# Splitting attention operands earlier and weights later in a float32 attention + MoE kernel

## The chip, the cores and the metric

The kernel runs on one core of a Trainium2 chip. The metric is the device time of one execution in microseconds (us); the kernel before takes 1088.51 us (median of 3 runs, 1087.3 to 1088.69).

## The reference, cut to what matters

Eight batches of eight heads attend over 32 global and 512 local positions with head dimension 64. The global queries see every position; a local query sees the 32 global positions and a band of 32 positions on either side. The result, 4352 rows of 512, goes through a two-layer network with a sigmoid gate. Everything is float32, and the weights come in as 64-bit floats.

```
s_g = scale * matmul(q_g, k_all.T);  out_g = matmul(softmax(s_g), v_all)
s_ll = where(abs(i - j) <= 32, scale * matmul(q_l, k_l.T), -1e9)
a_l = softmax(concat([scale * matmul(q_l, k_g.T), s_ll]))
x = concat([out_g, matmul(a_l, v_all)])        # (8*544, 512)
h = x @ w_in                                   # w_in: 512 x 2048
out = (h * (1 / (1 + exp(-h)))) @ w_out        # w_out: 2048 x 512
```

## The kernel before, in words

**Two kinds of product.** TensorE can multiply float32 operands as they are ("whole"), which the hardware does as two instructions for one matmul, or it can multiply rounded operands (type `F32R`). For the second kind each operand is split into a rounded high part and the rest, and a product is the sum of three: high by high, high by low, low by high. A whole operand is ready when it has been loaded. A split one first needs a cast on ScalarE (ACT) and a subtraction on VectorE (DVE) or GpSimd (POOL).

**Attention.** There are 128 local steps, numbered k: one step is a pair of heads for 128 queries of one batch, four steps make one tile of 128 rows. Each step loads q and k (`st_load`, L285) and v (`st_vload`, L293), splits them (`st_split`, L301; `st_vsplit`, L316), forms scores and softmax (`st_scores`, L327), transposes the probabilities (`st_turn`) and multiplies by v (`st_out`, L404). Steps with k below `KF` (24) are whole: `st_split` and `st_vsplit` return at once, the scores are one matmul for each head, and the probabilities are transposed where they stand. From `KF` on the scores are three products (for k below `ND` = 28), the probabilities are first moved by a DMA within SBUF into the tile `rr` (L365), of which there is one, and are then transposed; the transposed ones are split into `pt_hi` (ACT, L389) and `pt_lo` (DVE, L390), with the columns of the global queries added on POOL (L400, L401), and the product with v has six matmuls for a head where the whole form has two (each two-part). For k below 28 the subtractions for k (`klo`, L310) and v (`vlo`, L323) are on POOL. The global queries have steps of their own (`g_load`, `g_scores`, `g_soft`, `g_turn`), whole for the first two batches.

**The two-layer network.** The rows go through in 12 blocks of 2 or 3 tiles (`SIZES`). A block has 16 slices f of the hidden dimension: `first_layer(n, f)` forms h for 128 hidden units, ACT and DVE apply the gate, and one slice later `second_layer(n, f)` adds into the output. Block 0 is whole, with float32 weights `w_32`; the blocks from 1 on use the split weights `w_hi` and `w_lo`. A half slice of weights comes in by `load_weights` (L164): a DMA of 64-bit words into one of eight buffers `raw_w` (L171), a conversion on ACT (L179), and two integer operations on DVE (L181, L182). `split_weights(f)` (L185) makes the high part with two casts on ACT (L192) and the low part with two subtractions on POOL (L193); the tile of `w_lo[f]` takes the place of `w_32[f - 1]`, so the subtraction waits until block 0 is done with that.

**What sets the order.** The order of TensorE (PE) is written out: the planner gives each part of a step a due time, and `fill` hands out the parts that are due between the matmuls of the slices, so that attention for the next block runs inside the current one. Before block 0 the program issues the scores of steps 0 to 9, the transposes of steps 0 to 8 and the outputs of steps 0 to 7; block 0 then holds the outputs of steps 8 to 19, block 1 goes on with step 20. The other engines and the DMA queue of SP are ordered by the scheduler of the language, which takes the program order as priority and a simulated time for readiness, so an instruction can be placed well ahead of where the program has it. Each engine then works its list strictly in order.

**Places of the change.** `KF` (L41), `FIRSTW` (L46: the step from which, up to step 7, one `load_weights` is put at each step; what is still missing is loaded from slice 0 on, `LOOK` = 5 slices ahead), the call of `split_weights(f)` at the end of `second_layer` in block 0 (L592), and the main loop (L606).

Of the kernel before, what the change touches and what calls it, by code (L numbers as in the profile page):

```python
# [28 lines left out]
NCC, NF = DM // P, DFF // P  # L29
# [8 lines left out]
SIZES = (2, 3, 3, 3, 3, 3, 3, 3, 3, 3, 3, 2)  # L38
BUFS = dict(qk=2, raw=2, p=2, vraw=2, rr=1)
ND = 28  # L40
KF = 24  # L41
GF = 2
KP = 12
SCRATCH = 8
LOOK = 5
FIRSTW, PACE, WAT = 2, 1.0, -1.5  # L46

DUE = dict(load=-1.2, split=-0.5, vload=-0.6, vsplit=0.95, turn=1.6, out=2.2)
LAG = 2.25
# [9 lines left out]
def attention_moe_kernel(ctx: ExitStack, tc: tile.TileContext, qk0_in, qk_in, v_in, gqk, wts, out):  # L59
# [48 lines left out]
    def scratch(i, dtype, name):  # L108
        assert i not in taken
        return const.tile([P, 2 * DM], dtype, tag=f"wh{i}", name=name)  # L110


    probs = [const.tile([P, 2, 2 * P], F32, name=f"probs{i}") for i in range(BUFS["p"])]
    more = [scratch(SCRATCH - 1 - i, F32, f"probs{i}_") for i in range(2)]
    probs += [more[i // 2][:, DM * (i % 2) : DM * (i % 2 + 1)].rearrange("p (u j) -> p u j", u=2) for i in range(3)]
# [28 lines left out]
    def raw_tile(name, whole=False):  # L144
        some = SCRATCH - 4 not in taken
        i = next(homes) % (4 if some else 2) if whole else 0
        if i > 1:
            return scratch(SCRATCH - 1 - i, F32, name)
        if i:
            return work.tile([P, QW + KW], F32, tag="qk", bufs=BUFS["qk"], name=name)  # L150
        return raws.tile([P, QW + KW], F32, tag="raw", name=name)
# [10 lines left out]
    w_32, w_hi, w_lo, w_next = [], [], [], [0, 0]  # L162

    def load_weights():  # L164
# [4 lines left out]
        w = w_32[f][:, c0 : c0 + DM]  # L169
        raw = scratch(SCRATCH + (2 * f + c0 // DM) % (NF - SCRATCH), I32, f"raw_w{f}_{c0}")  # L170
        load = nc.sync.dma_start(out=raw, in_=wts[f, :, c0 : c0 + DM].bitcast(I32))  # L171
        if 2 * f + c0 // DM < NF - SCRATCH:
            tc.keep_in_program_order(load)
# [11 lines left out]
    def split_weights(f):  # L185
        taken.add(f)
        w_hi.append(const.tile([P, 2 * DM], F32R, tag=f"wh{f}", name=f"w_hi{f}"))
        w_lo.append(const.tile([P, 2 * DM], F32R, tag=f"ws{f}", name=f"w_lo{f}"))
        for c0 in range(0, 2 * DM, DM):
            sl = slice(c0, c0 + DM)  # L190
            hi, lo, w = w_hi[f][:, sl], w_lo[f][:, sl], w_32[f][:, sl]
            nc.scalar.copy(out=hi, in_=w)  # L192
            nc.gpsimd.tensor_tensor(out=lo, in0=w, in1=hi.bitcast(F32), op=ALU.subtract)  # L193
# [91 lines left out]
    def st_load(k, b, c, pr):  # L285
        raw = raw_tile(f"raw{k}", k < KF)
        if k < ND:
            nc.sync.dma_start(out=raw[:, : QW + W], in_=qk0_in[k])
        else:
            nc.sync.dma_start(out=raw, in_=qk_in[k - ND])  # L290
        tiles["raw", k] = raw

    def st_vload(k, b, c, pr):  # L293
        if k < KF and k % 2:
            vraw = two.tile([P, 2, 2, D], F32, tag="vhi" if k % 4 == 1 else "vlo", name=f"vraw{k}")
        else:
            vraw = raws.tile([P, 2, 2, D], F32, tag="vraw", bufs=BUFS["vraw"], name=f"vraw{k}")
        nc.sync.dma_start(out=vraw.rearrange("p a u d -> p (a u d)"), in_=v_in[b, c, pr])
        tiles["vraw", k] = vraw

    def st_split(k, b, c, pr):  # L301
        if k < KF:
            return
        raw = tiles.pop(("raw", k))
        qk, klo = qk_tiles(k)
        tiles["qk", k] = qk, klo
        if k < ND:
            n = QW + W
            nc.scalar.copy(out=qk[:, :n], in_=raw[:, :n])
            (nc.gpsimd if k < ND else nc.vector).tensor_tensor(out=klo[:, :n], in0=raw[:, :n], in1=qk[:, :n].bitcast(F32), op=ALU.subtract)  # L310
            return
        nc.scalar.copy(out=qk, in_=raw)  # L312
        (nc.gpsimd if k < ND else nc.vector).tensor_tensor(out=klo[:, :KW], in0=raw[:, QW:], in1=qk[:, QW:].bitcast(F32), op=ALU.subtract)
        nc.vector.tensor_tensor(out=qk[D:, :QW], in0=raw[D:, :QW], in1=qk[D:, :QW].bitcast(F32), op=ALU.subtract)

    def st_vsplit(k, b, c, pr):  # L316
        if k < KF:
            return
        vraw = tiles.pop(("vraw", k))
        vhi = two.tile([P, 2, 2, D], F32R, tag="vhi", name=f"vhi{k}")  # L320
        vlo = two.tile([P, 2, 2, D], F32R, tag="vlo", name=f"vlo{k}")
        nc.scalar.copy(out=vhi, in_=vraw)
        (nc.gpsimd if k < ND else nc.vector).tensor_tensor(  # L323
            out=vlo, in0=vraw, in1=vhi.bitcast(F32), op=ALU.subtract)
        tiles["v", k] = vhi, vlo

    def st_scores(k, b, c, pr):  # L327
        if k < KF:
            raw = tiles.pop(("raw", k))
# [3 lines left out]
        for u in range(2):  # L333
            o = s[:, u * W : (u + 1) * W]
            qs = slice(u * P, (u + 1) * P)
            if k < KF:
                terms = [(raw[:, qs], raw[:, QW : QW + W])]
# [212 lines left out]
    def first_layer(n, f):  # L550
        nt = SIZES[n] * P
        xh, xl = xblk[n]
        h = ps_h.tile([P, 512], F32, tag="h", name=f"h{n}_{f}")
        i = 0
        for c in range(NCC):
            if n == 0:
                nc.tensor.matmul(h[:, :nt], w_32[f][:, c * P : (c + 1) * P], xh[:, c, :nt], start=(c == 0),  # L557
                                 stop=(c == NCC - 1))
                continue
            wh = w_hi[f][:, c * P : (c + 1) * P]  # L560
            wl = w_lo[f][:, c * P : (c + 1) * P]
            for wt, x in ((wh, xh), (wh, xl), (wl, xh)):
                nc.tensor.matmul(h[:, :nt], wt, x[:, c, :nt], start=(i == 0), stop=(i == 3 * NCC - 1))  # L563
                i += 1
        t = two.tile([P, 3 * P], F32, tag="t", bufs=1, name=f"t{n}_{f}")
        gh = two.tile([P, 3 * P], F32R if n else F32, tag="gh", name=f"gh{n}_{f}")
        gl = two.tile([P, 3 * P], F32R, tag="gl", bufs=1, name=f"gl{n}_{f}") if n else None

        nc.scalar.activation(t[:, :nt], h[:, :nt], AF.Tanh, scale=0.5)  # L569
        out = t if n else gh  # L570
        nc.vector.scalar_tensor_tensor(out=out[:, :nt], in0=t[:, :nt], scalar=1.0, in1=h[:, :nt], op0=ALU.add,  # L571
                                       op1=ALU.mult)
        if n == 0:
            return gh, gl
        nc.scalar.copy(out=gh[:, :nt], in_=t[:, :nt])  # L575
        nc.vector.tensor_tensor(out=gl[:, :nt], in0=t[:, :nt], in1=gh[:, :nt].bitcast(F32), op=ALU.subtract)  # L576
        return gh, gl

    def second_layer(n, f, gh, gl):
        if f == 0:  # L580
            outs[n] = [ps_out.tile([P, DM], F32, tag=f"out{i}", name=f"out{n}_{i}") for i in range(SIZES[n])]
        wh, wl = (w_hi[f][:, DM:], w_lo[f][:, DM:]) if n else (w_32[f][:, DM : 2 * DM], None)
        for i, o in enumerate(outs[n]):
            sl = slice(i * P, (i + 1) * P)
            if n == 0:
                nc.tensor.matmul(o, gh[:, sl], wh, start=(f == 0), stop=(f == NF - 1))  # L586
            else:
                nc.tensor.matmul(o, gh[:, sl], wh, start=(f == 0), stop=False)  # L588
                nc.tensor.matmul(o, gh[:, sl], wl, start=False, stop=False)  # L589
                nc.tensor.matmul(o, gl[:, sl], wh, start=False, stop=(f == NF - 1))  # L590
            fill(1)
        if n == 0:  # L592
            split_weights(f)
        if f == NF - 1:
            while ("rg", 0) in state or ("rg", 1) in state:
                advance(stream[done][0])
            for i, o in enumerate(outs.pop(n)):
                sb = two.tile([P, DM], F32, tag="o", name=f"o{n}_{i}")
                nc.scalar.activation(sb, o, AF.Copy, scale=0.5)
                for p0, np_, r in out_rows(sum(SIZES[:n]) + i):  # L600
                    nc.sync.dma_start(out=out[r : r + np_, :], in_=sb[p0 : p0 + np_, :])
# [4 lines left out]
    for n in range(len(SIZES)):  # L606
        for f in range(NF):
            if n == 0:
                while tuple(w_next) < (min(NF, f + LOOK), 0):
                    load_weights()  # L610
            elif f == 0:
                advance(ends[n])
                now[:] = n, 0
            g = first_layer(n, f)
            fill(SIZES[n])
            if pend is not None:
                second_layer(*pend)
            pend = (n, f, *g)
    second_layer(*pend)


# [67 lines left out]
```

## Time and profile before

| | |
|---|---|
| median of the runs | 1088.51 us |
| profiled execution | 1086.34 us, of which span 1084.6 us |
| PE busy | 1053.5 us (97%) |
| DVE busy | 727.4 us (67%) |
| ACT busy | 693.0 us (64%) |
| POOL busy | 146.5 us (14%) |
| mean granted TensorE clock | 0.989 |
| moved by DMA | 127.29 MB |

The page gives the share of busy time, a picture of the span in 40 slices, the chain of work that ended last, and the costliest groups of instructions with the wait ahead of them. Chain and timeline rows read: start in us, length in us, engine, line, tile, and how often. A row of the busy table gives a stretch, its length, then for each engine busy us and number of instructions, the granted TensorE clock, the busy share of the DMA engines and GB/s.

### The profile page before, as it was taken

The page shows a single profiled execution, that of the slowest core. Times are in us where ns is not written, and L with a number is a line of the kernel's source. Part 1 is how long each engine was busy: PE and PEld are TensorE (multiplying, and loading weights), DVE is VectorE, ACT ScalarE, POOL GpSimd, SP SyncE. Part 2 cuts the span into 40 slices and gives each one's busy share as a digit, 9 for nine tenths or more (in the row PEclk, how much of TensorE's full clock was granted, in tenths as well). Part 3 has the DMA queues.
Part 4 walks back from the last instruction along what each step waited for, and adds up shares of the span by engine and source line. Part 5 has one row for each costly group of instructions (what it writes and reads, how often), then busy time and mean ns, then how long its engine had stood idle before and what let it go on. Part 6 is the DMA issues. An engine that isn't in the chain of part 4 may idle for free.

```text
span 1084.6 us, 20466 instructions
## 1 busy us (share of the span) xinstructions
PE 1053.5 (97%) x6568; PEld 934.9 (86%) x6568; DVE 727.4 (67%) x2367; ACT 693.0 (64%) x1845; POOL 146.5 (14%) x360
## 2 busy tenths in 40 slices
PE   6878999999999999999999999999999999999998
PEld 4645778989999999999999999998999999999997
DVE  5974355777677777666777877786778867753322
ACT  7875456767677766656766766776677776653232
POOL 3123542111100110000110100001000111000000
PEclk8989999999999999999999999999999999999999
DMA  9961112343334333332433433443344433310000
GB/s 351 380 189 59 57 59 76 119 146 125 111 112 142 124 107 115 116 115 82 140 110 122 149 111 109 138 135 108 111 141 125 141 114 112 112 60 20 1 30 20
DMA packets 69611, 127.29 MB, mean 117 GB/s; under 512 B 9344, under 2 KB 29312, under 8 KB 69504
## 3 DMA queue, kind: packets, MB, share of 16 engines
q1 hardware_dynamic: 69504, 125.99, 36.1%
q8 instruction: 52, 0.85, 0.3%
q14 instruction: 55, 0.45, 0.1%
HBM read 86.44 MB, written 8.91 MB: 88 GB/s over the span
## 4 chain that ended last, share of the span: by engine, by line
PE 93%; ACT 3%; DVE 2%; issue 1%; DMA 1%; ACTq 0%; DVEq 0%
PE h L563 33%; PE out L588 12%; PE out L590 11%; PE out L589 11%; PE o L423 10%; PE s L345 6%; PE t L380 3%; PE h L557 2%; PE out L586 2%; PE t L378 1%; DMA raw_w<-in_wts_dram 1%; PE gs L226 1%; PE gs L228 1%; ACT w_hi L192 1%; ACT w L179 1%
## 5 line engine op out<-in xcount | busy, mean ns | idle before, releaser
L563 PE MATMUL h<-xh,w_hi 128*128 128x384 f32 (+1 forms) x704 | 236.8, 336 | 0.0
L563 PE MATMUL h<-xh,w_lo 128*128 128x384 f32 (+1 forms) x704 | 233.5, 332 | 0.0
L563 PE MATMUL h<-xl,w_hi 128*128 128x384 f32 (+1 forms) x704 | 233.1, 331 | 0.0
L569 ACT ACTIVATE t<-h 128x384 f32<-128x384 f32 (+1 forms) x192 | 90.7, 472 | 207.3 <-PE h L563 189.4
L588 PE MATMUL out<-w_hi,gh 128*128 128x512 f32 x512 | 210.6, 411 | 0.0
L590 PE MATMUL out<-w_hi,gl 128*128 128x512 f32 x512 | 201.3, 393 | 0.0
L589 PE MATMUL out<-w_lo,gh 128*128 128x512 f32 x512 | 200.3, 391 | 0.0
L571 DVE SCALAR_TENSOR_TENSOR t<-t,h 128x384 f32<-128x384 f32 (+1 forms) x176 | 95.2, 541 | 132.6 <-ACT t L569 131.9
L563 PEld LDWEIGHTS h<-xl,w_hi 128*128 128x128 f32 x704 | 132.6, 188 | 5.4 <-issue 0.5
L563 PEld LDWEIGHTS h<-xh,w_hi 128*128 128x128 f32 x704 | 132.5, 188 | 5.4 <-issue 0.7
L400 POOL CAST pt_hi<-pgt 128x64 fp32r<-128x64 f32 (+1 forms) x132 | 39.1, 308 | 724.4 <-PE o L423 706.1
L563 PEld LDWEIGHTS h<-xh,w_lo 128*128 128x128 f32 x704 | 132.3, 188 | 0.0
L576 DVE TENSOR_TENSOR gl<-t,gh 128x384 fp32r<-128x384 f32 (+1 forms) x176 | 96.8, 550 | 46.6 <-PE out L590 42.5
L349 DVE CUSTOM_DVE_ANT_0 probs<-s,mask 128x224 f32<-128x224 f32 x244 | 85.0, 384 | 62.0 <-PE s L345 61.4
L353 ACT ACTIVATE probs<-probs,st 128x224 f32<-128x224 f32 x244 | 115.7, 475 | 11.2 <-DVE st L349 10.5
L590 PEld LDWEIGHTS out<-w_hi,gl 128*128 128x128 f32 x512 | 96.1, 188 | 22.3 <-DVE gl L576 0.3
L589 PEld LDWEIGHTS out<-w_lo,gh 128*128 128x128 f32 x512 | 97.0, 189 | 10.5
L588 PEld LDWEIGHTS out<-w_hi,gh 128*128 128x128 f32 x512 | 96.4, 188 | 10.6 <-ACT gh L575 0.4
L575 ACT CAST gh<-t 128x384 fp32r<-128x384 f32 (+1 forms) x176 | 88.3, 501 | 21.8 <-DVE t L571 17.3
L434 ACT CAST xh<-o 64x128 fp32r<-64x128 f32 x240 | 61.3, 256 | 42.5 <-PE o L423 29.4
L312 ACT CAST qk<-raw 128x704 fp32r<-128x704 f32 x100 | 78.2, 782 | 15.9 <-PE s L345 15.6
L435 DVE TENSOR_TENSOR xl<-o,xh 64x128 fp32r<-64x128 f32 x240 | 67.3, 280 | 30.9 <-ACT xh L434 27.4
(117 smaller groups left out, 1937.3 us busy)
## 6 DMA issues: line engine op xcount, KB each, us to landing
raw<-in_qk_dram SPq DMA_DIRECT2D x100, 352.0 KB, 3.0
rr<-probs SPq DMA_DIRECT2D x104, 256.0 KB, 2.3
raw_w<-in_wts_dram SPq DMA_DIRECT2D x32, 512.0 KB, 6.3
vraw<-in_v_dram SPq DMA_DIRECT2D x128, 128.0 KB, 2.4
raw_g<-in_gqk_dram SPq DMA_DIRECT2D x32, 304.0 KB, 2.9
out_dram<-o SPq DMA_DIRECT2D x32, 256.0 KB, 2.3
raw<-in_qk_dram SPq DMA_DIRECT2D x28, 240.0 KB, 4.8
rg<-pg SPq DMA_DIRECT2D x12, 256.0 KB, 2.4
```

What stands on the lines that cost most here:

```text
L312: nc.scalar.copy(out=qk, in_=raw)
L349: nc.vector.tensor_tensor_reduce(out=p[:, u, :W], in0=s[:, u * W : (u + 1) * W], in1=mask_of[c], scale=-SCALE, scalar=3.0e38, op0=ALU.add, ...
L353: nc.scalar.activation(p[:, u, :W], p[:, u, :W], AF.Exp, bias=st[:, u : u + 1], scale=-1.0, accum_out=st[:, 2 + u : 3 + u])
L423: nc.tensor.matmul(o[:D, u * wide : u * wide + m], v[:, a, u, :], pt[:, u, a, :m], start=(i == 0), stop=(i == len(terms) - 1))
L563: nc.tensor.matmul(h[:, :nt], wt, x[:, c, :nt], start=(i == 0), stop=(i == 3 * NCC - 1))
L569: nc.scalar.activation(t[:, :nt], h[:, :nt], AF.Tanh, scale=0.5)
L571: nc.vector.scalar_tensor_tensor(out=out[:, :nt], in0=t[:, :nt], scalar=1.0, in1=h[:, :nt], op0=ALU.add, op1=ALU.mult)
L575: nc.scalar.copy(out=gh[:, :nt], in_=t[:, :nt])
L576: nc.vector.tensor_tensor(out=gl[:, :nt], in0=t[:, :nt], in1=gh[:, :nt].bitcast(F32), op=ALU.subtract)
L588: nc.tensor.matmul(o, gh[:, sl], wh, start=(f == 0), stop=False)
L589: nc.tensor.matmul(o, gh[:, sl], wl, start=False, stop=False)
L590: nc.tensor.matmul(o, gl[:, sl], wh, start=False, stop=(f == NF - 1))
```

## The change

Three things are changed. Steps 8 to 23 take the split form instead of the whole one. Weights are loaded from step 4 instead of step 2 on, so four half slices instead of six are asked for before block 0, and the rest from slice 0 on. The weights of slice i are split not right after their use in block 0, but where 7 + 0.75 i slices have begun, counted through blocks 0 and 1: slice 0 at the start of the eighth slice, slice 10 in the last slice of block 0, slices 11 to 15 in the first four slices of block 1.

```
-KF = 24
+KF = 8
...
+SPLIT0, SPLITS = 7, 0.75
...
-FIRSTW, PACE, WAT = 2, 1.0, -1.5
+FIRSTW, PACE, WAT = 4, 1.0, -1.5
...
             fill(1)
-        if n == 0:
-            split_weights(f)
         if f == NF - 1:
...
             elif f == 0:
                 advance(ends[n])
                 now[:] = n, 0
+            while len(w_hi) < NF and SPLIT0 + SPLITS * len(w_hi) <= NF * n + f:
+                split_weights(len(w_hi))
             g = first_layer(n, f)
```

More of the change, by code (lines that the diff above doesn't have):

```diff
@@ L40 @@
 ND = 28
-KF = 24
+KF = 8
 GF = 2
@@ L44 @@
 SCRATCH = 8
+SPLIT0, SPLITS = 7, 0.75
 LOOK = 5
-FIRSTW, PACE, WAT = 2, 1.0, -1.5
+FIRSTW, PACE, WAT = 4, 1.0, -1.5
 DUE = dict(load=-1.2, split=-0.5, vload=-0.6, vsplit=0.95, turn=1.6, out=2.2)
@@ L591, in second_layer @@
             fill(1)
-        if n == 0:
-            split_weights(f)
         if f == NF - 1:
@@ L613, in attention_moe_kernel @@
                 now[:] = n, 0
+            while len(w_hi) < NF and SPLIT0 + SPLITS * len(w_hi) <= NF * n + f:
+                split_weights(len(w_hi))
             g = first_layer(n, f)
```

## The prediction

> **What bounds the kernel now.** I read the busy table by stages first, since the page's average for PE hides where the rest goes. The columns are the stretch, its length, busy time and instructions of PE, PEld, DVE, ACT and POOL, the granted clock, the DMA share and GB/s.
>
> ```profile
> 0.00:48.00 48.00, 34.33 (x168) 26.19 (x169) 34.57 (x132) 38.07 (x104) 11.39 (x34) 0.89 0.99 365
> 48.00:100.00 52.00, 41.99 (x156) 27.11 (x154) 34.33 (x94) 38.34 (x93) 12.53 (x16) 0.87 0.51 165
> 100.00:155.00 55.00, 54.25 (x251) 38.84 (x251) 28.36 (x104) 27.05 (x82) 27.34 (x32) 1.00 0.19 52
> 155.00:190.00 35.00, 35.00 (x197) 30.26 (x197) 16.90 (x59) 20.75 (x57) 10.47 (x15) 1.00 0.26 79
> 190.00:1084.00 894.00, 887.93 (x5801) 812.48 (x5800) 613.28 (x1981) 568.75 (x1513) 84.77 (x263) 1.00 0.34 107
> ```
>
> There are two kernels in one here. From 100 us on PE is the bound: it idles 0.75 us of 55, then nothing, and what shortens the time there is less PE work and nothing else. Before 100 us PE idles 13.7 us (first row, the work ahead of block 0) and 10.0 us (second row, the first six slices of block 0), at a clock below 0.9; there ACT, DVE and the DMA (99% busy up to 48) take turns.
>
> Next I asked what PE waits for from 45 to 160 us (line, releaser: us in total, times, longest), and what ACT did ahead of the first of these waits.
>
> ```profile
> PE o L423 <- issue: 4.3, 3, 3.2
> PE gs L226 <- DVE acc L442: 3.3, 1, 3.3
> PE o L423 <- ACT pg L231: 2.7, 1, 2.7
> ```
>
> ```profile
> 56.16 1.65 ACT L192 CAST w_hi<-w 128x512 fp32r<-128x512 f32 x3
> 57.70 0.38 ACT L231 COPY pg<-gs 64x272 f32<-64x272 f32 x1
> 58.10 0.26 ACT L434 CAST xh<-o 64x128 fp32r<-64x128 f32 x1
> ```
>
> Three waits of 3.3, 3.2 and 2.7 us make 9.2 us of the 10.0. In the first, PE wants a score bank that DVE frees once ACT has copied `xh`, and that copy stands behind three casts of weights. So the early part of block 0 hangs on small copies out of PSUM that queue behind weight work on ACT.
>
> ```profile
> 0.00:48.00 48.00, 3.64 (x6) 0.89 0.99 365
> 48.00:100.00 52.00, 13.76 (x24) 0.87 0.51 165
> ```
>
> These are the casts of L192 alone: 30 of 32 are over by 100 us, though the program asks for the last of them only at the end of block 0, which is in the fourth row of the busy table. The scheduler puts them as early as their data allow.
>
> **The change part by part. First, steps 8 to 23 become split.** Their price on PE is read from pieces of the chain in a stage where PE waits for nothing: whole steps first (`x4`, `x8`), split ones (`x6`, `x12`) behind.
>
> ```profile
> 157.51 0.76 PE s L345 x4
> ...
> 159.12 1.12 PE o L423 x8
> ...
> 163.39 0.44 PE t L378 x4
> ```
>
> ```profile
> 190.66 0.80 PE o L423 x12
> ...
> 192.21 0.66 PE s L345 x6
> ...
> 194.96 0.30 PE t L380 x4
> ```
>
> A whole step costs 0.76 + 1.12 + 0.44 = 2.32 us, a split one 0.66 + 0.80 + 0.30 = 1.76: more instructions, but 0.56 us less. How many steps lie where PE is the bound?
>
> ```profile
> L423 PE MATMUL o<-pt,vraw x96: 272/299/351, 100.0 to 182.9; 128*64 128x160 f32 x64, 128*64 128x128 f32 x32
> ```
>
> From 98 to 186 us there are 96 instructions of whole outputs, eight a step: 12 steps, 12 to 23. They give 12 x 0.56 = 6.7 us, my firmest term. The four steps 8 to 11 lie in the stage that waits anyway; at nothing for them the term is 6.7, at full worth 16 x 0.56 = 9.0. I take 6.7.
>
> The split costs other engines time. These groups are from the stretch where the first split steps of the kernel before run, steps 24 and on (mean ns of one is the number before the last bar):
>
> ```profile
> L322 ACT CAST vhi<-vraw 128x256 fp32r<-128x256 f32 x6 | 2.4, 406 | 0.0
> L309 ACT CAST qk<-raw 128x480 fp32r<-128x480 f32 x4 | 2.4, 596 | 1.2 <-PE s L345 1.0 <-POOL pt_lo L126 0.2
> ```
>
> ```profile
> L310 POOL TENSOR_TENSOR klo<-raw,qk 128x480 fp32r<-128x480 f32 x4 | 4.9, 1214 | 11.4 <-ACT qk L309 11.4
> ...
> L323 POOL TENSOR_TENSOR vlo<-vraw,vhi 128x256 fp32r<-128x256 f32 x4 | 3.3, 818 | 2.6 <-ACT vhi L322 2.6
> ...
> L390 DVE TENSOR_TENSOR pt_lo<-t,pt_hi 128x512 fp32r<-128x512 f32 x4 | 2.7, 680 | 0.0
> ```
>
> Each step adds 0.41 + 0.60 = 1.0 us on ACT, 1.2 + 0.8 = 2.0 us on POOL and 0.7 us on DVE. From 100 us on ACT is busy 27.05 of 55 and DVE 28.36 of 55, so PE's work covers both; without that cover 12 steps would cost 12 us on ACT.
>
> **Second, the DMA that a split step adds.** Softmax now ends in a DMA into `rr`, and the transpose waits for it. The tile `rr` exists once, as do `pt_hi` and `pt_lo`, so a step's DMA waits for the transposes of the step before, and behind that DMA on SP stand the loads of later steps and weights. In the last row of the busy table, where every step has this form, PE idles 6 us of 894, so a step's own spacing covers it. Step 8 is different: its transpose is the last thing PE does before block 0.
>
> ```profile
> 45.88 0.48 ACT L357 ACTIVATE probs__116<-probs__116,st 128x224 f32<-128x224 f32 x1
> ```
>
> ```profile
> 47.23 0.59 PE t L378 x4
> ```
>
> ```profile
> raw_w<-in_wts_dram SPq DMA_DIRECT2D x10, 512.0 KB, 6.1
> ```
>
> ```profile
> rr<-probs SPq DMA_DIRECT2D x104, 256.0 KB, 2.3
> ```
>
> Its probabilities are scaled at 45.88 + 0.48 = 46.36 us and transposed at 47.23. Between 35 and 60 us the queue is full and a weight transfer takes 6.1 us to land (third row); over the whole kernel a DMA into `rr` takes 2.3 (fourth). At 6.1 the transpose comes at 52.5, 5.2 us late; at 2.3 it comes at 48.7, 1.4 us late. Since six casts (3.64 us of ACT) can leave the stretch ahead, the step may also come up sooner, so the bounds are 1.4 - 3.6 = -2.2 and +5.2. Everything of block 0 is queued on PE behind this transpose. But while PE stands, ACT and DVE go on with weights and catch up, and the next three waits are for them, so part is given back: I take half of the worse end, +2.6.
>
> **Third, the weight splits move back.** In the stretch 48 to 100 us ACT would lose up to 13.8 us of casts and take on six steps' operands (10 to 15), 6 x 1.0 = 6.0 us: a net relief of 7.8 us. Nothing of it counts if the scheduler still hoists the casts; all of it could go into the 9.2 us of waits. I take half, -3.9, because the new place in the program gives the casts a lower priority, but the row of 30 hoisted casts shows that the place alone does not fix when they run. The bounds are 0 and -9.2. Where the casts go, after 100 us, they are hidden by PE's 54.25 us of 55 and 35.00 of 35: ACT has 28 and 14 us free there, against at most 3.64 + 13.76 = 17.4 us of casts and 8 x 1.0 = 8.0 us of operands for steps 16 to 23. The subtractions on POOL go with the casts; by then block 0 is done with the tile that they write to, so they wait for nothing more, and a split issues no DMA. The first weight that block 1 needs is slice 0 in slice 16, nine slices after its split is asked for, and each later one has more room.
>
> **Fourth, two weight loads fewer ahead of block 0.** No wait of PE names a weight, the DMA is 99% busy in whatever order, and all halves still have to come; each is one DMA on SP, one conversion on ACT and two operations on DVE, wherever it stands. I cost it at nothing; what hides it is that same full queue, and without that cover it is the two conversions that block 0 would find undone.
>
> The sum is -6.7 + 2.6 - 3.9 = -8.0 us against the profiled execution's 1086.34 (span 1084.6 and 1.7 around it): 1078.3. The median of the runs, 1088.51, lies 2.2 us above that execution, so I forecast 1088.5 - 8.0 = 1080.5.
>
> **The rivals. A, the early stage clears up wholly.** All 9.2 us of waits go, and the late transpose is made good by them: -6.7 - 9.2 = -15.9, 1072.6. For it: the waits have one cause. Against it: ACT takes on step operands in the same place.
>
> **B, the casts stay where they are.** Then ACT is no freer, the transpose of step 8 costs its 5.2 us, and -6.7 + 5.2 = -1.5 gives 1087.0, within 0.2%. For it speak the 30 hoisted casts: the splits would be moved in the program and not in time. Against it: in the crowded stage a lower priority should lose.
>
> **C, slower: the `rr` transfers queue behind weight loads.** SP issues its DMAs strictly in order, and weight loads wait there for a free buffer:
>
> ```profile
> SPq L171 <- DVE w L182: 12.5, 4, 6.1
> ```
>
> That is 3.1 us a time between 35 and 100 us. If the transfers of steps 9, 10 and 11, whose transposes lie among the last weight loads, each come 3.1 us late into PE's fixed order, that is 9.4 us besides the 5.2 of step 8: -6.7 - 3.9 + 5.2 + 9.4 = +4.0, 1092.5. It decides once each of the three is later than (6.7 + 3.9 - 5.2) / 3 = 1.8 us. Against it: these transposes lie a slice or more behind their scores.
>
> **D, POOL becomes the bound of block 0's second half.** From 100 to 155 us it is busy 27.34 us of 55, for the greater part with subtractions for weights, which the change leaves in this stage. With steps 12 to 19 it gets 8 x 2.0 = 16 us more: 43 of 55. And POOL and DVE hold each other up:
>
> ```profile
> 61.53 2.94 POOL L193 TENSOR_TENSOR w_lo<-w,w_hi 128x512 fp32r<-128x512 f32 x2 [7.60 <-PE out L586]
> ```
>
> ```profile
> 61.69 1.65 DVE L182 SCALAR_TENSOR_TENSOR w<-w,raw_w 128x512 uint32<-128x512 uint32 x1 [0.91 <-ACT w L179]
> 63.27 1.49 DVE L181 TENSOR_SCALAR raw_w<-raw_w 128x512 uint32<-128x512 uint32 x1
> 65.63 0.69 DVE L182 SCALAR_TENSOR_TENSOR w<-w,raw_w 128x512 uint32<-128x512 uint32 x1 [0.87 <-ACT w L179]
> ```
>
> The DVE operation that takes 0.69 us alone takes 1.65 beside POOL's subtraction, 0.96 more. If one such hold a step reached PE in steps 12 to 19, 8 x 0.96 = 7.7 us would eat the gain: -0.3, 1088.2, no change. The Trainium skill has this as a rule, in "SBUF — State Buffer", section "Who interferes with whom": a DVE instruction with two SBUF inputs contends with a GpSimd instruction that reads SBUF, and the shared port pair is locked for a whole instruction. The trace agrees (1.65 against 0.69 us), and by the rule the new subtractions on POOL would collide too. What speaks against it as the bound is that DVE has half of that stage free.
>
> **How the numbers follow.** The forecast has 0.50, A 0.18, B 0.10, D 0.07, C 0.15. A measurement of this kernel can tell some 0.2%, 2.2 us, from no change: faster is below 1086.3, slower above 1090.7. The forecast and A make faster 0.68, B and D make same 0.17, C makes slower 0.15. The forecast's own range is 1075 to 1086 (it would take the second and third terms both near an end of their bounds to leave it). The range for 8 in 10 runs from 1070, below A, to 1092, just short of C's time, and leaves out about half of C and the far tail of A.
>
> **What would show it.** The term on PE is right if a step in block 0 shows 0.66, 0.80 and 0.30 us after 100 us and PE busy falls by about 9 us over all 16 steps; it is wrong if PE is no longer full there. The late transpose shows as a wait of PE for a DMA into `rr` ahead of the first first-layer matmul, at up to 5 us. The relief shows as fewer than 24 casts of L192 between block 0's start and its sixth slice, and waits under 9.2 us; B shows as the same 24. C shows as waits for `rr` in the first four slices, D as POOL above 80% in the second half of block 0 with PE waiting for `klo`, `vlo` or `pt_lo`. The forecast is wrong if block 0 as a whole gets longer.

## The result

The changed kernel takes 1103.59 us (median of four runs, 1101.61 to 1104.8). The kernel before took 1088.17 beside it. The ratio is 1.0138, with an interval of 1.0122 to 1.0155: slower by 15.4 us, where 8 us less were forecast, and outside the range. The profiled execution took 1104.3 us, its span 1102.5, which is 17.9 more than before.

### The profile page after: what moved, and what is told of

Same layout as the page of the kernel before. It is cut to its first block, busy times and chain, and to the rows that moved or that the text cites. A ratio compares the mean times of both kernels' runs of the same rounds, so it can differ in the third digit from the quotient of the medians.

```text
span 1102.5 us, 20895 instructions
## 1 busy us (share of the span) xinstructions
PE 1049.4 (95%) x6664; PEld 935.2 (85%) x6664; DVE 751.9 (68%) x2383; ACT 706.3 (64%) x1877; POOL 184.0 (17%) x408
## 4 chain that ended last, share of the span: by engine, by line
PE 90%; issue 2%; DMA 2%; DVE 2%; ACT 2%; POOL 1%; SPq 0%; DVEq 0%; ACTq 0%; POOLq 0%
PE h L564 32%; PE out L589 11%; PE out L591 11%; PE out L590 11%; PE o L424 10%; PE s L346 6%; PE t L381 3%; PE h L558 2%; PE out L587 2%; DMA raw_w<-in_wts_dram 1%; DMA rr<-probs__116 1%; PE gs L229 1%; PE gs L231 1%; PE gs L230 1%; DMA raw<-in_qk_dram 1%
## 5 line engine op out<-in xcount | busy, mean ns | idle before, releaser
L401 POOL CAST pt_hi<-pgt 128x64 fp32r<-128x64 f32 (+1 forms) x152 | 44.8, 307 | 757.7 <-PE o L424 739.4
L577 DVE TENSOR_TENSOR gl<-t,gh 128x384 fp32r<-128x384 f32 (+1 forms) x176 | 96.6, 549 | 46.3 <-PE out L591 42.1
L350 DVE CUSTOM_DVE_ANT_0 probs<-s,mask 128x224 f32<-128x224 f32 x244 | 85.1, 385 | 62.6 <-PE s L346 61.7
L424 PE MATMUL o<-pt_hi,vhi 128*64 128x160 f32 x480 | 93.6, 240 | 8.5 <-ACT pt_hi L390 7.2
L391 DVE TENSOR_TENSOR pt_lo<-t,pt_hi 128x512 fp32r<-128x512 f32 x120 | 82.7, 689 | 11.3 <-ACT pt_hi L390 11.0
L424 PE MATMUL o<-pt_hi,vlo 128*64 128x160 f32 x480 | 88.4, 233 | 0.0
```

The source lines that it names most:

```text
L350: nc.vector.tensor_tensor_reduce(out=p[:, u, :W], in0=s[:, u * W : (u + 1) * W], in1=mask_of[c], scale=-SCALE, scalar=3.0e38, op0=ALU.add, ...
L391: nc.vector.tensor_tensor(out=pt_lo[:, :, :, :P], in0=t4, in1=pt_hi[:, :, :, :P].bitcast(F32), op=ALU.subtract)
L424: nc.tensor.matmul(o[:D, u * wide : u * wide + m], v[:, a, u, :], pt[:, u, a, :m], start=(i == 0), stop=(i == len(terms) - 1))
```

## The profile after

**The busy table by stages**, with the same columns and stretches as in the prediction (stretch, length, PE, PEld, DVE, ACT, POOL, granted clock, DMA share, GB/s):

```profile
0.00:48.00 48.00, 31.96 (x158) 23.82 (x158) 34.69 (x118) 37.57 (x101) 15.45 (x37) 0.93 0.88 303
48.00:100.00 52.00, 33.85 (x145) 22.91 (x146) 39.06 (x99) 39.57 (x93) 21.04 (x26) 0.74 0.68 226
100.00:155.00 55.00, 42.67 (x232) 31.07 (x231) 31.66 (x83) 27.56 (x79) 33.40 (x46) 0.91 0.23 70
155.00:190.00 35.00, 35.00 (x222) 28.26 (x221) 23.31 (x74) 23.14 (x66) 24.57 (x31) 1.00 0.41 127
```

The third row overturns the forecast. PE idled 0.75 us of these 55 and now idles 12.3. The second row is worse too, 18.2 us idle where there were 10.0. POOL is busier in all four rows, yet at 33.40 of 55 it is far from full. After 190 us PE is as full as before.

**What PE waits for** in the first 190 us (line, releaser: us in total, times, longest):

```profile
PE t L381 <- DMA rr<-probs__116: 9.7, 1, 9.7
...
PE o L424 <- ACT pt_hi L390: 7.2, 1, 7.2
PE gs L227 <- DVE acc L443: 6.8, 2, 3.7
...
PE s L346 <- ACT pgt L281: 3.1, 2, 2.4
```

The first two are new. The first is step 8's transpose, the second the output of a step in the eighth slice. The start of a slice's first matmul, read from PE's timeline, shows what each is worth:

| start, us | slice 0 | slice 7 | slice 8 | slice 10 | block 1 | end |
|---|---|---|---|---|---|---|
| before | 47.66 | 103.82 | 109.88 | 120.38 | 154.86 | 1084.6 |
| after | 60.43 | 112.77 | 127.11 | 139.66 | 173.61 | 1102.5 |
| later by | 12.8 | 9.0 | 17.2 | 19.3 | 18.8 | 17.9 |

So 12.8 us are lost ahead of block 0, 3.8 are given back by slice 7, 8.3 are lost in one slice and 2.1 in the next two. Only 1.4 is gained behind that.

**The first place.** The chain of waits from 44 to 61 us, and what POOL did at its head (start, length, engine, tile, line):

```profile
45.57 0.60 DVE w L183
46.17 1.93 DVE raw_w L182
...
48.19 1.03 DVE w L183
...
52.12 0.39 ACT probs__116 L358
52.50 0.07 ACT x L431
52.57 7.20 DMA rr<-probs__116
59.78 0.14 issue
59.91 0.72 PE t L381 x4
60.63 1.41 PE h L558 x3
```

```profile
46.00 1.24 POOL L311 TENSOR_TENSOR klo<-raw,qk 128x480 fp32r<-128x480 f32 x1 [1.92 <-ACT qk L310]
47.18 0.62 POOL L127 MEMSET pt_hi<- 128x640 f32 x1
47.80 0.87 POOL L324 TENSOR_TENSOR vlo<-vraw,vhi 128x256 fp32r<-128x256 f32 x1
```

Two delays are in series. The probabilities of step 8 are scaled at 52.51 us, not at 46.36, and then the DMA into `rr` takes 7.20 us. The first delay has two parts. PE begins the scores of step 8 at 43.91 us instead of 41.96, and from there to the scaled probabilities it takes 8.6 us instead of 4.4. In this second part POOL makes the low parts of early steps' k and v. Beside them the DVE operation of L182 (L181 before, 0.43 to 0.47 us between 41 and 45 us) takes 1.93 us of the chain. Further down, in rows left out here, ACT does two casts of weights (1.13 us), the exponentials of step 9 (1.03) and a cast of a later step's q and k (0.48) ahead of step 8's last scaling.

**The second place.** DVE's timeline, then POOL's over the same time, then PE's:

```profile
111.50 0.26 DVE L436 TENSOR_TENSOR xl<-o,xh 64x128 fp32r<-64x128 f32 x1
111.69 0.17 DVE L443 TENSOR_TENSOR acc<-o,acc 64x32 f32<-64x32 f32 x1
111.79 8.67 DVE L251 TENSOR_SCALAR pg<-pg,gst 128x544 f32<-128x544 f32 x1
...
120.89 0.39 DVE L350 CUSTOM_DVE_ANT_0 probs<-s,mask 128x224 f32<-128x224 f32 x1
```

```profile
110.01 1.28 POOL L194 TENSOR_TENSOR w_lo<-w,w_hi 128x512 fp32r<-128x512 f32 x1 [4.04 <-ACT w_hi L193]
111.24 0.40 POOL L401 CAST pt_hi<-pgt 128x64 fp32r<-128x64 f32 x2
111.61 1.26 POOL L194 TENSOR_TENSOR w_lo<-w,w_hi 128x512 fp32r<-128x512 f32 x1
...
116.53 1.18 POOL L311 TENSOR_TENSOR klo<-raw,qk 128x480 fp32r<-128x480 f32 x1
117.68 2.47 POOL L194 TENSOR_TENSOR w_lo<-w,w_hi 128x512 fp32r<-128x512 f32 x2
```

```profile
123.91 0.36 PE L424 MATMUL o<-pt_hi,vhi 128*64 128x160 f32 x1 [7.16 <-ACT pt_hi L390]
```

In the kernel before, the DVE operation that scales `pg` took 0.50 and 0.48 us in batch 1 (at 79.22 and 102.40). Here the second of the two takes 8.67. From 110.01 to 120.15 POOL's rows follow each other with no idle time (each begins where the one above ends), and the DVE operation ends 0.3 us behind the last. Below, such a stretch of POOL's work is called an unbroken run, and an operation that stands beside it is called held. Softmax of the running step (L350) stands behind it on DVE, then come operations on ACT and DVE, the last of them the cast to `pt_hi`, and the output that needs it is next in PE's order.

Not every unbroken run holds DVE to its end. In the same kernel POOL works from 135.37 to 143.10 us without idle time as well (DVE first, POOL behind it):

```profile
136.84 1.10 DVE L359 TENSOR_SCALAR probs<-probs,st 128x224 f32<-128x224 f32 x1
```

```profile
135.37 1.20 POOL L311 TENSOR_TENSOR klo<-raw,qk 128x480 fp32r<-128x480 f32 x1 [3.07 <-PE o L424]
136.53 2.53 POOL L194 TENSOR_TENSOR w_lo<-w,w_hi 128x512 fp32r<-128x512 f32 x2
```

This DVE operation, 0.34 us elsewhere, is let go at 137.94, 5.2 us ahead of the end of the run. So the length of such a run is what a hold can cost, not what it must cost.

## The experiments

The theory taken to the chip: the split steps lose the time, in two places. Step 8 reaches its transpose late, and DVE is held beside unbroken runs of POOL. The main rival was that the moved weight splits did it. Times are medians; "before" is the kernel before in the same session, and a gain or loss is the difference to it.

**One part alone.** Only the split steps, with weights as before:

```
-KF = 24
+KF = 8
```

> Steps 8 to 23 split, weights as before. Theory: the loss has two places, the DMA into rr ahead of block 0 (block 0 begins some 12 us late) and a DVE operation held for 8.7 us behind a train of POOL subtractions, which needs the late weights; so this kernel keeps the first loss, is free of the second and gets the PE work of 12 steps (-6.7): about 1088.5 + 12 - 6.7 = 1094. Rival, that the late weights are the whole loss: about 1082.

1104.17 us beside 1087.91, ratio 1.0162 (1.0145 to 1.0179): +16.3, all of the loss and not the share that I gave it. Two rows of its timelines:

```profile
52.23 0.72 PE L380 MATMUL t<-ident,rr 128*128 128x128 f32 x4 [3.54 <-DMA rr<-probs__116]
...
109.89 7.12 DVE L250 TENSOR_SCALAR pg<-pg,gst 128x544 f32<-128x544 f32 x1
```

The transpose is late by less, but the same DVE operation is held, 7.12 us. So the hold doesn't need the moved splits.

Only the moved weight splits: the changed kernel with the old steps and loads.

```
-KF = 8
+KF = 24
...
-FIRSTW, PACE, WAT = 4, 1.0, -1.5
+FIRSTW, PACE, WAT = 2, 1.0, -1.5
```

> Weight splits late, steps whole to 23 and weight loads from step 2 as before. Theory: without subtractions for klo and vlo POOL forms no long train, and ACT has fewer casts early, so nothing is lost: 1084 to 1089. Rival, that the late weights are the whole loss: 1096 or more.

1089.84 us, ratio 1.0022 (1.0012 to 1.0033): +1.9. The rival falls. So does my third term: this part alone brings nothing and costs a little.

Only the later loads: the kernel before with

```
-FIRSTW, PACE, WAT = 2, 1.0, -1.5
+FIRSTW, PACE, WAT = 4, 1.0, -1.5
```

> The kernel before with weights from step 4 on, nothing else. Theory: no wait of PE hangs on it, 1086 to 1090. Rival, that the conversions missing at the start of block 0 cost: 1092 or more.

1081.94 us beside 1087.72, ratio 0.9945 (0.9924 to 0.9966): 5.8 us faster, which neither theory had. In the kernel before, two pieces of the chain in block 0 are weights that are waited for:

```profile
72.67 4.29 DMA raw_w<-in_wts_dram
...
82.09 3.94 DMA raw_w<-in_wts_dram
```

In this kernel's chain no DMA stands between 60 and 100 us, slice 6 begins at 91.6 us instead of 96.6, and block 1 at 149.9 instead of 154.9. The weights as a whole don't come sooner: the 20th of the 32 conversions on ACT (L179) begins at 59.0 us instead of 53.4, the last at 84.8 instead of 86.0. That the chain had these two pieces shows the place; why the order of asking does this was not tried further.

The three parts alone make +16.3 + 1.9 - 5.8 = +12.4, and the whole change +15.4. So they don't quite add up, by 3 us.

**How many split steps.** The changed kernel with steps 8 and 9 whole, and with step 8 alone whole:

```
-KF = 8
+KF = 10
```

> The changed kernel with steps 8 and 9 whole again. Theory: no DMA into rr stands ahead of block 0, so the wait of 9.7 us there goes and block 0 begins 9 to 12 us earlier: 1092 to 1096. Rival, that ACT and DVE have to do the same work anyway and the wait only moves into the first slices: 1101 to 1105.

1087.89 us beside 1087.91, ratio 0.9996 (0.9981 to 1.001). Both losses go, not the first alone as expected: block 0 begins at 49.2 us, and no operation on DVE takes 3 us.

```
-KF = 8
+KF = 9
```

> The changed kernel with step 8 alone whole again. Theory: only the transpose of step 8 stands ahead of block 0, so block 0 begins by 50 us as it does with steps 8 and 9 whole, and the time is within 4 us of that kernel's 1087.9. Rival, that the wait goes over to the next transfer, that of step 9, whose transpose comes in the first slice: 1096 to 1104.

1086.53 us beside 1087.72, ratio 1.0001 (0.9986 to 1.0017). One step out of sixteen turns +15.4 into nothing. The page's totals of this kernel (busy us, share, instructions) show what the other fifteen bring:

```profile
PE 1043.4 (96%) x6658; PEld 929.8 (86%) x6658; DVE 745.6 (69%) x2382; ACT 704.9 (65%) x1875; POOL 184.1 (17%) x405
```

PE has 10.1 us less to do than before (1053.5), two thirds of a microsecond a step, and the time stays the same: the gain is there, and waits take it back (slice 0 begins at 51.7 us, 4.0 later and not by 50 as expected, and block 1 at 157.1, 2.3 later). More is taken back than that shows: this kernel also has the later loads, which alone brought 5.8 us.

Why the hold is gone as well can be read in the kernel with `KF` = 10, DVE first, POOL behind it:

```profile
108.98 2.17 DVE L356 TENSOR_SCALAR st<-st 128x2 f32<-128x2 f32 x1 [0.90 <-ACT probs L354]
```

```profile
109.94 1.18 POOL L311 TENSOR_TENSOR klo<-raw,qk 128x480 fp32r<-128x480 f32 x1
111.29 2.53 POOL L194 TENSOR_TENSOR w_lo<-w,w_hi 128x512 fp32r<-128x512 f32 x2 [0.16 <-POOL klo L311]
```

POOL idles 0.16 us from 111.13 on, and DVE's operation ends at 111.15. A gap that short is enough. The scaling of `pg` itself is not held in this kernel: it starts at 106.16 us, 0.03 ahead of POOL's `vlo`, and takes 0.48, while `vlo` takes 1.05 instead of 0.72. Why the operations fall this way in some kernels and not in others (block 0 begins earlier in these) was not tried by itself.

**Step 8 without its DMA.** Split products, but the probabilities of step 8 transposed where they stand:

```
+KD = 9
...
-        if k < KF:
+        if k < KD:
...
+        direct = k < KD
...
-        if whole:
+        if direct:
```

> The changed kernel, with step 8 split as in it, but transposed straight from its probabilities, without the DMA into rr. Theory: the trip through the full DMA queue is what holds block 0 back, not the casts and subtractions of step 8: block 0 begins by 52 us, and the time is 1086 to 1096 (the lower end if the long hold of DVE goes with it, as it does with step 8 whole). Rival, that the other work of the split step is late as well: block 0 begins after 57 us, 1100 or more.

1094.37 us beside 1088.9, ratio 1.0049 (1.003 to 1.0068): +5.5. Block 0 begins at 56.0 us, between the two expectations. Without the DMA 60.4 - 56.0 = 4.4 us of the 12.8 go, and 8.4 remain. The 4.4 is a net figure, since the scores of step 8 begin at 46.28 us here and at 43.91 in the changed kernel. The chain to the transpose shows 1.94 and 1.02 us on DVE's L183 and L184 beside POOL, which take 0.43 and 0.69 alone. That is 1.8 us; the scores come 4.3 us later than in the kernel before, and ACT again has other work ahead of the last scaling. So DVE beside POOL has a part in the 8.4, and how large the whole of POOL's part is was not separated. The long hold stays, to the hundredth:

```profile
105.71 8.68 DVE L252 TENSOR_SCALAR pg<-pg,gst 128x544 f32<-128x544 f32 x1
```

**Is it that DVE operation?** Its two instances in batch 1 moved to ACT:

```
-        nc.vector.tensor_scalar(out=pg, in0=pg, scalar1=st[:, 3:4], scalar2=None, op0=ALU.mult)
+        if b == 1:
+            nc.scalar.activation(pg, pg, AF.Copy, scale=st[:, 3:4])
+        else:
+            nc.vector.tensor_scalar(out=pg, in0=pg, scalar1=st[:, 3:4], scalar2=None, op0=ALU.mult)
```

> The changed kernel with one operation moved: the scaling of pg (L251) of batch 1 goes to ACT. Theory: DVE's operation of 8.67 us was held by the port that it shares with POOL; on ACT it takes under 1 us, and the wait of 7.2 us of PE at 117 to 124 us goes: about 1095.5. Rival, that POOL's train holds the next DVE operation just as long: 1102 to 1105.

1102.27 us beside 1087.91, ratio 1.0138 (1.0122 to 1.0153). No gain, and the reason is one row, with the last of POOL's below it:

```profile
113.74 5.55 DVE L359 TENSOR_SCALAR st<-st 128x2 f32<-128x2 f32 x1 [0.80 <-ACT probs L357]
```

```profile
116.78 2.47 POOL L194 TENSOR_TENSOR w_lo<-w,w_hi 128x512 fp32r<-128x512 f32 x2
```

The next operation of the same kind is held, and this one has two elements to a partition. It ends at 119.29, POOL at 119.25. So it isn't this one operation, nor its size: the next one that stands beside the same run of POOL is held to its end. Not every DVE operation is held: `xl` and `acc`, which read `o` in PSUM, took 0.26 and 0.17 us with POOL running beside them.

The Trainium skill, "SBUF — State Buffer", section "Who interferes with whom", lists tensor_scalar among the instructions that can take the port pair that DVE shares with GpSimd; whichever issues first has it for a whole instruction, and the other blocks fully. The rows agree on who is held and who isn't. On how long, they go beyond it: one POOL instruction lasts 1.3 us, and the holds last 5.55 to 8.68.

**POOL's share taken away.** The subtractions for k and v of steps 8 to 27 on DVE itself:

```
-            (nc.gpsimd if k < ND else nc.vector).tensor_tensor(out=klo[:, :n], ...
+            nc.vector.tensor_tensor(out=klo[:, :n], ...
```

> The changed kernel with the subtractions for klo and vlo of steps 8 to 27 on DVE instead of POOL. Theory: POOL's unbroken train at 110 to 120 us consists of weight subtractions and those of the steps; without the latter it has gaps, no DVE operation is held for more than about 1.5 us, and the second loss of about 10 us goes while the wait for rr stays: 1092 to 1096. Rival, that DVE has no room for them: 1101 or more.

1097.71 us beside 1087.72, ratio 1.0094 (1.0076 to 1.0113): +10.0, so 5.4 of the loss go, a little less than expected. The wait for `rr` ahead of block 0 is still 9.7 us. From slice 7 to block 1 it takes 52.4 us instead of 60.8, and the longest operation on DVE there is 2.98 us. The reason in the theory doesn't fit, though: POOL still works from 110.22 to 119.40 us with no idle time of 0.1 us or more, and yet two held operations of DVE get through inside it, after 1.66 and 2.98 us. So taking the subtractions away shortened the holds; by what means stays open.

The same with `KF` = 10 (both edits above):

> Steps 10 to 23 split, and klo and vlo of steps 10 to 27 on DVE. Theory: neither of the two losses is left, and the PE work of steps 12 to 23 (-6.7) shows: 1080 to 1084, faster than both kernels. Rival, that DVE becomes late in block 0: 1088 or more.

1083.43 us, ratio 0.996 (0.9944 to 0.9976): 4.3 us faster than before, as expected in time. But the later loads alone took 1081.94 us in the same session, so this doesn't show the gain on PE: the split steps and late weight splits together bring nothing on top of the loads.

**What is best.** The kernel before with `FIRSTW` = 4 and splits from step 16 on:

```
-KF = 24
+KF = 16
...
-FIRSTW, PACE, WAT = 2, 1.0, -1.5
+FIRSTW, PACE, WAT = 4, 1.0, -1.5
```

> The kernel before with weights from step 4 on and steps 16 to 23 split, weight splits as before. Theory: eight steps at 0.56 us less PE work each, all behind 100 us where PE is the bound, give -4.5 against the 1081.9 of the kernel with the later loads alone: 1077 to 1079. Rival, that POOL's subtractions hold DVE and eat it: 1081 or more.

1079.32 us beside 1088.9, ratio 0.9909 (0.9893 to 0.9926). Its third row of the busy table:

```profile
100.00:155.00 55.00, 53.71 (x301) 39.87 (x300) 31.86 (x107) 33.68 (x100) 45.15 (x54) 1.00 0.27 82
```

POOL is busier than in the changed kernel, 45.15 us of 55 against 33.40, PE is nearly full, and no DVE operation between 100 and 155 us takes over 1.3 us. POOL even works from 138.33 to 148.06 us without a pause of 0.01 us, almost as long as in the run of the 8.67, and the longest DVE operation beside it takes 1.04. Neither POOL's share of busy time nor the length of its run tells whether it does harm.

With the subtractions for k and v on DVE as well:

> The same with klo and vlo of steps 16 to 27 on DVE. Theory: the price on PE as above and no holds: 1076 to 1078, up to 1 us below the one with POOL. Rival, that POOL has gaps enough with eight steps: the same within 1 us.

1076.37 us, ratio 0.9889 (0.9873 to 0.9904): faster than both kernels, by 12.5 us than before. Its interval touches that of the run above it, so the 3 us between the two aren't settled.

And with splits from step 10 on:

> The same with steps 10 to 23 split. Theory: steps 12 to 15 add -2.2, steps 10 and 11 lie where PE waits anyway: 1074 to 1077. Rival, that split steps in the early stage cost more on ACT and DVE than they bring: 1079 or more.

1083.16 us, ratio 0.9951 (0.9938 to 0.9965). Six more split steps cost 6.8 us. In the profiled executions, which lie 4.1 us apart, slice 2 begins 3.7 us later and block 1 only 2.3: much of the loss falls at the start of block 0, in the stage where PE waits for others, and some of it behind block 0.

## Why the prediction was wrong

**First term, -6.7: right on PE, with its cover gone.** Split steps cost what was read from the later stage, here in the chain behind 175 us:

```profile
176.26 0.66 PE s L346 x6
...
177.79 0.81 PE o L424 x12
...
181.59 0.30 PE t L381 x4
```

That is 1.77 us a step against 1.76 forecast. Where little else moves it arrives: splits from step 16 on bring 9.6 - 5.8 = 3.8 us against 8 x 0.56 = 4.5, which the intervals don't tell apart. In the changed kernel it doesn't, because the term rested on PE being full from 100 us on, with ACT and DVE covered by its work, and PE idles 12.3 us of 55 there. That cover is the second step that failed: an engine busy half of the time can still be late in one place, and the 8.3 us lost in the eighth slice had no term in the sum.

**Second term, +2.6: the step that failed first.** The prediction let the probabilities of step 8 be ready at 46.36 us or sooner and gave the DMA up to 6.1 us. They were ready at 52.51, and the DMA took 7.20. The size of the DMA was nearly right; the upper bound of 5.2 broke mainly on the other part. It asked what ACT would be relieved of ahead of block 0, and put the operands of steps 8 and 9, which ACT and POOL now have to make there, at nothing without a reason. The transpose came 12.7 us late: 1.95 by the start of the step's scores, 4.2 from there to the scaled probabilities, 6.5 from there to the transpose, the DMA and its wait. How much of the first two is POOL's work beside DVE stays open; without the DMA block 0 still began 8.4 us late. "Part is given back" did hold, 3.8 us by slice 7, but whether through work that caught up or through the later loads was not separated.

**Third term, -3.9: nothing came.** It took the later place in the program to move half of the casts. These are the casts of L193 alone, by stretch:

```profile
48.00:100.00 52.00, 13.03 (x22) 0.74 0.68 226
100.00:155.00 55.00, 2.29 (x4) 0.91 0.23 70
```

There are 22 of them in the stretch that had 24. Counted as the prediction asked, from the start of block 0 to its sixth slice, 18 begin where there were 24, but only because 12 instead of 6 had begun before block 0, the other six at 49.25 us and later, most of them while PE stood. So they were not moved back in time, as rival B had it, and the part alone cost 1.9 us.

**Fourth term, 0: it was -5.8.** The prediction argued that no wait of PE named a weight. The chain of waits named two, of 4.29 and 3.94 us; PE's waits name only the last releaser (DVE and ACT), and the chain goes on to what held those.

**Rival D had the mechanism and not the price.** It took one hold, 1.65 - 0.69 = 0.96 us, and multiplied by steps. A held operation can wait for a whole unbroken run of POOL's operations: 8.67 - 0.50 = 8.2 us in one piece. That D's total, 8 x 0.96 = 7.7 us, lies near this is luck. What spoke against D, that DVE has half of that stage free, is no argument, since an engine that stands is late however much it has free. Its sign, POOL above 80%, wasn't seen (61%).

**Rivals A and C.** A's waits didn't clear. C had a loss but not its place: the transposes of steps 9 to 11 are not among PE's waits for `rr`, only step 8's is.

The causes that the runs show: step 8 split costs the difference between +15.4 and nothing (`KF` = 9); the late start falls by 4.4 us without its DMA; the holds of 5.55 to 8.68 us end with POOL's run in all four kernels that have them, and the hold moves on to another operation when the held one is taken away; taking k's and v's subtractions from POOL shortens it. Not shown: what made the 8.4 us that remain ahead of block 0, and why some runs of POOL hold DVE to their end and others as long let it go. With k's and v's subtractions on DVE the wait for `rr` stayed at 9.7 us, so it doesn't hang on their being on POOL; DVE then has them to do itself.

## What to carry to other kernels

Price a contention between two engines at up to the longest unbroken run of the neighbour's work, not at one instruction, and look for who stands behind the held instruction. Take that as the upper bound, and read from the trace whether it comes to it; shares of busy time say nothing about it. Before adding a round trip to a step, ask whether it is the last thing ahead of a barrier: there one step of sixteen turned a change that broke even into a loss of 15.4 us. Time the parts of a change alone: here the one costed at nothing was the only one that paid by itself, and the costliest paid, together with the later loads, once its first eight steps were left out.

## What the runs showed of the hardware

A tensor_scalar of 128x2 elements, 0.17 us elsewhere, took 5.55 us beside POOL, and one of 128x544 took 8.67, 7.12 and 8.68 instead of 0.50. In each case it ended 0.0 to 0.3 us behind POOL's last operation of the run, and a gap of 0.16 us in POOL's work was enough to let one through. A tensor_scalar of 128x1 (L247, at 110.08 us, inside a POOL subtraction from 110.01 to 111.29) took 0.15 us and was not held. Holds also end inside a run: at 46.09 us in the changed kernel after 2.00 us with POOL still at work (a memset lies there), at 136.84 after 1.10, at 165.61 after 1.03, 7.2 us ahead of the run's end. The trace has one difference. In the run of the 8.67 us, from the held operation on, each POOL instruction is recorded as starting 31 or 32 ns ahead of the end of the one before; where the operations of 136.84 and 165.61 were let go, it is 40 and 42 ns. Whether that is what lets DVE go wasn't tried.

The DMA into `rr`, 2.3 us in the median, took 7.20 behind four weight loads issued from 49.08 us on. In the two stretches where PE stands longer, the mean granted clock is lower too: 0.74 between 48 and 100 us after 0.87, and 0.91 between 100 and 155 after 1.00 (ahead of 48 us it is the other way, 0.93 after 0.89, with less PE work). Behind the wait of 9.7 us the eight matmuls of slice 0 took 3.74 us at a granted clock of 0.50 (60.0 to 64.2 us), against 2.27 in the kernel before (clock 1.00) and 1.89 where PE is full. Behind the wait of 7.2 us the clock is 0.50 again, from 124 to 128 us. So these waits cost more than their length.
